# Normalising finished rows on VectorE inside the second attention, and splitting the output weights there in pieces

## The chip, the cores and the metric

The kernel runs as one program on one core of a Trainium2 chip. The metric is the device time of one execution in microseconds (us). Three runs of the kernel before gave a median of 2710.52 us (2707.95 to 2712.14). A change of 0.2% is 5.4 us.

The engines are TensorE (PE, with its weight loads PEld), VectorE (DVE), ScalarE (ACT), GpSimd (POOL) and SyncE (SP). Matrix products are written to PSUM, and DVE or ACT bring them to SBUF. In this kernel DMAs are issued by SP and by POOL.

## The reference

A sequence of 2048 positions with 640 channels passes through four layers, each with a residual: attention, convolution, attention, convolution. Both attentions use the same weights, and both convolutions the same kernel.

```python
x = x + A(layernorm(x), wqkv, wo)   # 32 heads of 20 channels
x = x + B(layernorm(x), ...)        # S4D
x = x + A(layernorm(x), wqkv, wo)
x = x + B(layernorm(x), ...)

A: softmax(q @ k.T * 20 ** -0.5) @ v, heads side by side, @ wo
B: K[d, l] = 2 * Re(sum over n of C[d, n] * exp(A[d, n] * dt[d] * l)), l = 0 .. 2047
   y = irfft(rfft(u, 4096) * rfft(K, 4096))[:2048] + u * D_skip
```

`layernorm` takes mean and variance over the 640 channels of a position, and has no weights.

## The kernel before, in words

A tile of `x` is 128 partitions by 16 rows by 640 channels; "row s" below is one of these 16 (128 positions, 640 channels). Head groups `g` of four heads (8 groups) and query blocks `qb` of 512 positions (4) make the 32 turns of an attention. In a turn, 16 steps over the keys each do two score products on PE (`scores`, line 833), two exponentials of 128x1024 on ACT, and the products with the values on PE (`values`, line 850), which accumulate in `pa`.

**The order of work in an attention is written out by hand.** A `Plan` keeps a clock for PE, ACT and DVE, in units of about one us. After each score product, `fill` puts other pieces of work into PE's gaps as `slot` finds room. A list `later` holds small pieces with a due time, which `drain_later` emits once the plan's PE clock has passed it. While `plan.keep` is set, DVE, ACT, and the DMAs of POOL and SP keep the order in which they were emitted. POOL's arithmetic is not held to that order, and neither is anything behind the attention: there the framework's scheduler sets the order of each engine's queue at build time. Each queue runs in order.

**End of a turn.** `values` copies `pa` to `oc` on DVE. The last row of each head in `oc` holds the sums of the exponentials. They go out to DRAM (`dn<-oc`), come back spread over 128 partitions (`dr<-dn`), are inverted on DVE, go out (`dn<-dr`) and come back broadcast (`db<-dn`). All these DMAs are issued by POOL. Then `scale` multiplies `oc` by `db` on DVE, and `store` sends the block out (`ot<-oc`, POOL). For most turns `scale` is kept until the end of the next turn (`scaled`); for the last two head groups of the second attention it has the due time `plan.dve + 22`.

**Output weights.** Once the projections are done, `end_jobs` (line 905) calls `prefetch` (line 1076), which loads the output weights in five pieces of 128x640 (`wot`, SP) and splits each into a high and a low part, `woh` and `wol`, with a copy (line 1092) and a subtraction (line 1093) on POOL. In the first attention the load of `x` follows, in four DMAs, the last three of them through `later`. In the second attention `end_jobs` also takes a maximum over partitions on POOL, and four small operations on DVE behind it.

**Rows in the second attention.** Its last eight turns alternate between groups 6 and 7. During them `rows_out` (line 970) begins with the output projection: it loads a part of a row (`otl<-ot`, SP; channel tiles 0 to 2, or 3 and 4), splits it on DVE into `oh` and `ol`, multiplies on PE (line 997, three products for each pair), adds to `x` on DVE, and for a row with both parts done takes the statistics of the norm (`mvx`). Such a row is "whole".

**Behind an attention**, `out_proj` (line 1183) does the remaining rows in order (lines 1210 and 1215), with the split's copy on ACT. It calls `ln` for a pair of rows when they are ready, and in the second attention for one whole row after each step. `ln_u` (line 1098) makes `u`, its f16 high part `uh` (ACT) and its low part `ul` (line 1111: POOL, except for the last row). In the first layer `u` is made on DVE, in the second on ACT. In the first layer `ktransform` (line 1120), the transform of the convolution kernel, is woven in; its constants and its input `kl` are loaded by SP. Then `ssm` runs the convolution, whose first stage (line 1279) reads `uh` and `ul`.

Of the kernel before, what the change touches and what calls it, by code (L numbers as in the profile page):

```python
# [21 lines left out]
P = 128  # L22
L = 2048
D = 640
NI = L // P
NCT = D // P
# [11 lines left out]
LG = 2  # L38
BOUND = 30.0
SCALE = DH ** -0.5  # L40
EPS = 1e-5
# [45 lines left out]
def mha_s4d_kernel(ctx, tc, x_in, wqkv, wo, lar, aim, cr, ci, ldt, dsk,  # L87
                   c_e1, c_eb, c_f2, c_fa, c_sel, c_lv, c_id, c_sg, c_e16, c_f16, c_id16, out, parts="asas", general=None):
    nc = tc.nc
    plan = Plan()  # L90
# [42 lines left out]
    flag = cp.tile([P, 2], F32, name="flag")  # L133
# [268 lines left out]
    def attention(x, stats):  # L402
# [439 lines left out]
        def values(qb, g, kt, pts, pa):  # L842

            V = Vt[g // 2 % 3]
            plan.on_pe(0.865)
            for r in range(2):
                rows = slice(64 * r, 64 * r + 64)
                for j in range(4):
                    h = 4 * (g % 2) + j
                    chain(te.matmul(pa[r][32 * j:32 * j + 32, :], V[rows, kt, VP * h:VP * h + 32],  # L850
                                    pts[j // 2][rows, 512 * (j % 2):512 * (j % 2) + 512],
                                    start=(kt == 0), stop=(kt == NI - 1), tile_position=(64 * r, 32 * j)))
            if kt == NI - 1:
# [12 lines left out]
                def sums():  # L866
                    for j in range(4):
                        ge.dma_start(rows[j:j + 1, :], oc[32 * j + DH:32 * j + DH + 1, :])

                def load():  # L870
                    ge.dma_start(dr, dn[0, blk])

                def invert():
                    ve.tensor_scalar_max(dr, dr, 1e-30)
                    ve.reciprocal(dr, dr)

                def back():
# [12 lines left out]

                def store():
                    for j in range(4):
                        h = 4 * g + j
                        ge.dma_start(ot[h * DH:(h + 1) * DH, 512 * qb:512 * qb + 512], oc[32 * j:32 * j + DH, :])
                    stored[blk] = plan.pe
                later.extend((plan.dve + n, f) for n, f in (
                    (0.2, sums), (5.0, load), (10.0, invert), (11.0, back), (15.5, spread)))
                later.extend((plan.dve + n, lambda: slow and slow.pop(0)[1]()) for n in (18.0, 21.0, 24.0))
                if first_layer or g < H // 4 - 2:
                    scaled.append(scale)  # L900
                else:
                    later.append((plan.dve + 22.0, scale))
                later.sort(key=lambda e: e[0])

        def end_jobs():

            while filler[0] is not None:
                while slot():
                    pass
                weave(1)  # L910
            if not first_layer:
                wx = sm.tile([P, 2], F32, name="wx")
                ve.reduce_max(wx[:, 0:1], wm, axis=AX.X)
                ge.partition_all_reduce(wx[:, 1:2], wx[:, 0:1], P, bass.bass_isa.ReduceOp.max)
                ve.tensor_max(flag[:, 0:1], flag[:, 0:1], wx[:, 1:2])
                ve.reciprocal(wx[:, 0:1], wx[:, 1:2])
                ve.tensor_scalar_mul(wx[:, 0:1], wx[:, 0:1], 2.0 ** -4)
                ve.tensor_max(flag[:, 0:1], flag[:, 0:1], wx[:, 0:1])
            qc_.close()
            if not first_layer:  # L920
                xpools.pop().__exit__(None, None, None)
            rest = []
            made = prefetch(x, rest)
            later.extend((plan.pe + 8.0 + 3.0 * n, f) for n, f in enumerate(rest))
            later.sort(key=lambda e: e[0])
            return made

# [12 lines left out]
        class Rows:  # L940
# [21 lines left out]
            def pick(self):  # L962
                for c in (3, 0):
                    for item in self.left:
                        s, c0, c1 = item
                        if c0 == c and (c == 0 or all(4 * g + s // 4 in stored for g in (H // 4 - 2, H // 4 - 1))):
                            self.left.remove(item)
                            return item

        def rows_out(rows, x, woh, wol):  # L970

            def ask():
# [1 line left out]
                if item:  # L974
                    rows.load(item)
                return plan.pe + 6.0
            t, done, parts_done = plan.pe + 26.0, [], set()
            while rows.left or rows.loaded:
                yield t, 0.0, False, ()
                if stop:  # L980
# [26 lines left out]
                if s in parts_done:  # L1007
                    stats_of(x, s, rows.mv[:, s, :])
                    rows.whole.add(s)
                parts_done.add(s)  # L1010

        last[0] = None
# [63 lines left out]
    def prefetch(x, rest):  # L1076

        if x is None:
            xp = tc.tile_pool(name="xp", bufs=1, side="right")
            xpools.append(xp)  # L1080
            x = xp.__enter__().tile([P, NI, D], F32, name="x")
            for i in range(0, NI, 4):
                rest.append(lambda i=i: sy.dma_start(x[:, i:i + 4, :], xv[:, i:i + 4, :]))
        c = ExitStack()
        w1 = c.enter_context(tc.tile_pool(name="wo1", bufs=1, side="right"))
        woh = w1.tile([P, NCT, D], F32R, name="woh")
        wol = w1.tile([P, NCT, D], F32R, name="wol")
        with tc.tile_pool(name="wos", bufs=NCT, side="right") as ws:
            for ct in range(NCT):
                wt = ws.tile([P, D], F32, name="wot")  # L1090
                sy.dma_start(wt, wo[ct * P:ct * P + P, :])
                ge.tensor_copy(woh[:, ct, :], wt)
                ge.tensor_sub(wol[:, ct, :], wt, woh[:, ct, :])
        if rest:
            rest.pop(0)()
        return x, c, woh, wol, c.enter_context(tc.tile_pool(name="wo2", bufs=2, side="right"))

    def ln_u(x, i0, n, mvrs, uh, ul, pool, on_act=False):
        mv, rs = mvrs
# [83 lines left out]
    def out_proj(x, woh, wol, rows, first, ln):  # L1183
# [8 lines left out]
        assert whole == list(range(len(whole)))  # L1192
        rows.left.sort()
        feed()
        if whole:
            rsw = rstd(rows.mv[:, :len(whole), :], len(whole), rows.w2, "rsw")
        to_come = {s: 0 for s in range(NI)}
        for s, c0, c1 in rows.left + [e[0] for e in rows.loaded + first]:
            to_come[s] += 1

        def next_whole():
            if whole:
                s = whole.pop(0)
                ln(s, 1, (rows.mv[:, s:s + 1, :], rsw[:, s:s + 1]))
        while first:
            (s, c0, c1), oh, ol = first.pop(0)
            pos = [pst("M", [P, 512], F32, tag="mm", name="po")[:, :320] for _ in range(2)]
# [4 lines left out]
            for hf in range(2):  # L1212
# [18 lines left out]

    def ssm_consts(c):
# [230 lines left out]
    def seq(x, general):  # L1463

        stats = None
        for n in range(0, len(parts), 2):
            with ExitStack() as c:
# [10 lines left out]
                    psum(c3, M=2, T=2, F=2)  # L1478
                else:
                    psum(c3, M=4)  # L1480
                up = c.enter_context(tc.tile_pool(name="up", bufs=1))
                uh = up.tile([P, NI, D], F16, name="uh")
                ul = up.tile([P, NI, D], F16, name="ul")
                consts = ssm_consts(c)
                with ExitStack() as c2:
                    up2 = c2.enter_context(tc.tile_pool(name="up2", bufs=2 + n))

                    def ln(i0, m, mvrs=None):
                        ln_u(x, i0, m, mvrs or ln_stats(lambda i: x[:, i0 + i, :], m), uh, ul, up2, n > 0 and not general)
# [11 lines left out]
                psum(c, M=2, T=2, F=2)  # L1501
                end = n + 2 >= len(parts)
                stats = ssm(x, uh, ul, consts, end)
        return x

    xpools = []
# [81 lines left out]
```

## Time and profile before

| what | value |
|---|---|
| median of 3 runs | 2710.52 us (2707.95 to 2712.14) |
| the profiled execution | 2711.66 us |
| its span, first to last instruction | 2709.8 us |
| mean granted TensorE clock | 0.991 |
| ACT busy / PE busy | 2351.0 us / 2546.7 us |
| DVE busy / POOL busy | 1489.5 us / 849.7 us |

By stages, in us from the span's start: the first attention ends at about 1101, its output projection with the kernel transform reaches to about 1290, the first convolution to about 1499 together with the start of the second attention, which ends at about 2493; the second output projection lasts to about 2565, and the second convolution to the end.

How to read it: a row of a timeline has the start in us, the length in us, the engine, the line, the operation and its tiles, and in brackets the idle time of the engine before it with what ended that. Most helpers appear as line 77. A "q" behind an engine's name stands for its queue: issues of DMAs and waits. "issue" means that the engine waited for nothing that the profile shows.

### The profile page before, as it was taken

Reading aid. Unit: us, or ns where it says so; the run is one execution under the profiler, and the core shown is the slowest. Engines: PE = TensorE matmul, PEld = TensorE weight load, DVE = VectorE, ACT = ScalarE, POOL = GpSimd, SP = SyncE. Lnnn points to the kernel's source line nnn. Section 1 sums busy time; section 2 is a strip of 40 time slices with the busy share of each in tenths; the row PEclk is TensorE's granted clock in tenths of the full one; section 3 lists DMA queues with packets and bytes.
Section 4 is the critical chain, followed back from the end, with each engine's and each line's share of the span. In section 5 each row is a group of like instructions: output and inputs, shape, how many; then the busy total and the mean of one; then the engine's idle time right before and its main releaser. Section 6 shows DMA issues by size and latency. Waiting matters only on the chain.

```text
span 2709.8 us, 115874 instructions
## 1 busy us (share of the span) xinstructions
PE 2546.7 (94%) x50944; PEld 1439.3 (53%) x50944; DVE 1489.5 (55%) x3324; ACT 2351.0 (87%) x2772; POOL 849.7 (31%) x1282
## 2 busy tenths in 40 slices
PE   7899999999999988999999999999999998999798
PEld 3445444444444433777896544454454443444788
DVE  8677877777856992567776333232233221123765
ACT  7799999999999999455655899999999999998564
POOL 1132333232323334300671122222222224222476
PEclk9999999999999999999999999999999999999999
DMA  6522232322221224455542111111121113222365
GB/s 213 173 61 75 63 79 56 80 67 62 65 54 47 55 70 141 149 194 190 185 157 63 49 51 53 51 55 44 46 62 40 51 39 89 66 68 88 105 191 162
DMA packets 186787, 244.48 MB, mean 90 GB/s; under 512 B 43488, under 2 KB 128992, under 8 KB 184480
## 3 DMA queue, kind: packets, MB, share of 16 engines
q1 hardware_dynamic: 149936, 190.38, 22.1%
q0 software_dynamic: 36336, 46.59, 7.6%
q8 instruction: 402, 6.59, 1.0%
q14 instruction: 113, 0.93, 0.1%
HBM read 160.80 MB, written 76.03 MB: 87 GB/s over the span
## 4 chain that ended last, share of the span: by engine, by line
ACT 51%; PE 26%; issue 10%; DVE 7%; DMA 5%; POOL 1%; SPq 0%; ACTq 0%; DVEq 0%; POOLq 0%
ACT pt L77 49%; PE pa L850 4%; PE psy L1324 3%; PE psv L1314 3%; PE S L833 2%; PE psx L1302 2%; PE psx L1279 2%; PE po L1215 1%; PE m L586 1%; PE pst L1289 1%; PE pkf L1169 1%; DMA kop<-ks 1%; PE pq L739 1%; PE pkx L1152 1%; PE po L1210 1%
## 5 line engine op out<-in xcount | busy, mean ns | idle before, releaser
L77 ACT ACTIVATE pt<-S 128x1024 f32<-128x1024 f32 x2048 | 1929.1, 1033 | 48.7 <-PE S L833 35.5
L850 PE MATMUL pa<-pt,V 64*32 64x512 f32 x16384 | 1102.7, 591 | 0.7 <-DVE oc L77 0.6
L833 PE MATMUL S<-qop,kop 61*32 61x512 f16 x16384 | 882.2, 381 | 88.9 <-ACT pt L77 67.9
L833 PEld LDWEIGHTS <-kop 61*32 61x32 f16 x16384 | 367.2, 90 | 746.0 <-issue 620.3
L850 PEld LDWEIGHTS pa<-pt,V 64*32 64x32 f32 x16384 | 315.0, 106 | 73.7 <-issue 9.4
L77 POOL DMA_DIRECT2D dn<-oc x256 | 125.9, 498 | 662.9 <-DVE oc L77 610.2
L77 DVE TENSOR_SCALAR qc<-m 128x512 f32<-128x512 f32 (+1 forms) x68 | 46.8, 689 | 309.5 <-PE m L586 309.5
L77 POOL DMA_DIRECT2D db<-dn x256 | 129.2, 511 | 141.5 <-DMA dn<-dr 138.2
L586 PE MATMUL m<-xh,wh 64*32 64x512 f16 x2560 | 147.7, 379 | 2.2 <-DVE qc L77 2.0
L77 POOL DMA_DIRECT2D ot<-oc x256 | 129.8, 515 | 62.1 <-DVE oc L77 53.6
L586 PE MATMUL m<-xh,wl 64*32 64x512 f16 x2560 | 147.7, 378 | 0.0
L586 PE MATMUL m<-xl,wh 64*32 64x512 f16 x2560 | 146.0, 377 | 0.0
L77 DVE COPY oc<-pa 128x512 f32<-128x512 f32 x64 | 44.2, 690 | 183.4 <-PE pa L850 175.7
L586 PEld LDWEIGHTS <-wh 64*32 64x32 f16 x5120 | 92.6, 94 | 76.0 <-issue 33.5
L1307 POOL TENSOR_TENSOR t<-t,kb 128x512 f32<-128x512 f32 x80 | 101.9, 1275 | 70.2 <-DVE t L77 69.1
L77 ACT COPY xt<-pst 128x1024 f16<-128x1024 f16 x80 | 81.6, 1023 | 46.9 <-PE pst L1289 46.7
L77 POOL DMA_DIRECT2D dn<-dr x64 | 35.7, 558 | 245.9 <-DVE dr L77 236.8
L77 DVE TENSOR_SCALAR V<-m 128x160 f32<-128x160 f32 x64 | 20.7, 324 | 161.1 <-PE m L552 161.1
L77 DVE TENSOR_TENSOR kb<-ktab 128x512 f32<-128x512 f32 x160 | 106.4, 684 | 0.0
L552 PEld LDWEIGHTS <-xh 128*128 128x128 f16 x960 | 79.6, 98 | 48.0 <-issue 32.6
L1308 POOL TENSOR_TENSOR t<-t,t 128x512 f32<-128x512 f32 x78 | 99.2, 1271 | 7.3 <-DVE t L77 1.3
L323 PEld LDWEIGHTS m<-kb,ka 128*32 128x32 f32 x3840 | 61.0, 109 | 72.2 <-issue 56.6
(280 smaller groups left out, 3990.7 us busy)
## 6 DMA issues: line engine op xcount, KB each, us to landing
ka<-kha SPq DMA_DIRECT2D x80, 256.0 KB
kb<-khb SPq DMA_DIRECT2D x80, 256.0 KB
db<-dn POOLq DMA_DIRECT2D x256, 64.0 KB, 2.8
kop<-ks SPq DMA_DIRECT2D x176, 80.0 KB
kpw<-wd POOLq DMA_DIRECT2D x60, 192.0 KB, 4.9
qop<-qs SPq DMA_DIRECT2D x256, 40.0 KB
ot<-oc POOLq DMA_DIRECT2D x256, 40.0 KB, 2.9
kha<-kn SPq DMA_DIRECT2D x20, 512.0 KB
```

Of the source, the lines that this page charges most:

```text
L77: made = f(out, *a, **k)
L323: chain(te.matmul(ps[32 * j:32 * j + 32, c8, :], a[n][:, ch, :], b[n][:, dd, :], start=(n == 0), stop=(n == 2), tile_position=(0, 32 * j)))
L552: chain(te.matmul(ps[:, :n], a_[:, ct, sl], m[:, ct, :], start=(k == 0), stop=(k == 14)))
L586: chain(te.matmul(ps[r][32 * t:32 * t + 32, :], a_[rows, ct, 32 * u:32 * u + 32], m[rows, ct, 512 * v:512 * v + 512], start=(k == 0), stop ...
L833: chain(te.matmul(S[32 * t:32 * t + 32, 512 * r:512 * r + 512], kt_[rows, kc + 32 * t:kc + 32 * t + 32], qt[rows, :], start=True, stop=Tru ...
L850: chain(te.matmul(pa[r][32 * j:32 * j + 32, :], V[rows, kt, VP * h:VP * h + 32], pts[j // 2][rows, 512 * (j % 2):512 * (j % 2) + 512], sta ...
L1279: te.matmul(ps[:, r, i, :], e1[:, e, s, r, :], m[:, s, bs], start=(n == 0), stop=(n == 2))
L1302: te.matmul(px, f2[:, f, :], xt[:, k, :], start=(n == 0), stop=(n == 2))
L1307: ge.tensor_mul(t2, t2, kb)
L1308: (ge if g0 else ve).tensor_add(t1, t1, t2)
L1314: te.matmul(pv[:, g].rearrange("p r i c -> p (r i c)"), t1[:, g * P:g * P + P], fa, start=True, stop=True)
L1324: te.matmul(py[:, i, :], eb[:, 4 * i4 + i, r, :], v[:, r, 4 * i4 + i].rearrange("p g c -> p (g c)"), start=(r == 0), stop=(r == 1))
```

## The change

1. `scale` of the last two groups of the second attention is due at `plan.dve + 27` instead of 22.
2. The four small DVE operations behind the maximum in `end_jobs` go into `later`, six units on.
3. `prefetch` no longer uses POOL. The weights are loaded into the two buffers `otl` that the row loads use. Five pieces `halves`, one every four units, each copy and subtract on DVE, and issue the load of the next but one weight. The DMAs of `x` in the first attention come behind these pieces.
4. `rows_out` begins at 30 units instead of 26.
5. `normalise`: when a row is whole, DVE computes the inverse root from the bits of the variance and three Newton steps, then `u`, `uh` and `ul`. The five pieces are due 1.2 units apart. For this `uh` and `ul` of the second layer are allocated when the weights are.
6. `out_proj` calls `ln` only for rows that are not whole. In the second layer each call comes one step later in program order than before.

```diff
-                    later.append((plan.dve + 22.0, scale))
+                    later.append((plan.dve + 27.0, scale))
...
-                ve.tensor_max(flag[:, 0:1], flag[:, 0:1], wx[:, 1:2])
-                ve.reciprocal(wx[:, 0:1], wx[:, 1:2])
...
+                def bounds():
+                    ve.tensor_max(flag[:, 0:1], flag[:, 0:1], wx[:, 1:2])
...
+                later.append((plan.pe + 6.0, bounds))
...
-            later.extend((plan.pe + 8.0 + 3.0 * n, f) for n, f in enumerate(rest))
+            later.extend((plan.pe + 8.0 + 4.0 * n, f) for n, f in enumerate(rest))
...
+        def normalise(rows, x, s):
+            mv = rows.mv[:, s, :]
+            va, y, t = (sm.tile([P, 1], F32, tag=f"nr{n}", name=f"nr{n}") for n in range(3))
+            uh, ul = ups
+            def first_guess():
+                ve.tensor_scalar_add(va, mv[:, 1:2], EPS)
+                yi = y.bitcast(mybir.dt.int32)
+                ve.tensor_single_scalar(yi, va.bitcast(mybir.dt.int32), 1, ALU.logical_shift_right)
+                ve.tensor_single_scalar(yi, yi, 0x7FFFFFFF, ALU.bitwise_xor)
+                ve.tensor_scalar_mul(y, y, 0.679 * 2.0 ** -65)
+            def newton():
+                ve.tensor_mul(t, y, y)
+                ve.tensor_mul(t, t, va)
+                ve.tensor_scalar(t, t, -0.5, 1.5, ALU.mult, ALU.add)
+                ve.tensor_mul(y, y, t)
+            def parts():
+                u = rows.w2.tile([P, D], F32, bufs=1, name="u")
+                ve.tensor_scalar(u, x[:, s, :], mv[:, 0:1], y, ALU.subtract, ALU.mult)
+                ve.tensor_copy(uh[:, s, :], u)
+                later.append((plan.dve + 0.5, lambda: ve.tensor_sub(ul[:, s, :], u, uh[:, s, :])))
+                later.sort(key=lambda e: e[0])
+            later.extend((plan.dve + 1.2 * (n + 1), f) for n, f in enumerate((first_guess, newton, newton, newton, parts)))
+            later.sort(key=lambda e: e[0])
...
-            t, done, parts_done = plan.pe + 26.0, [], set()
+            t, done, parts_done = plan.pe + 30.0, [], set()
...
+                    normalise(rows, x, s)
...
+        else:
+            upx = tc.tile_pool(name="upx", bufs=1, side="right")
+            xpools.append(upx)
+            upx_ = upx.__enter__()
+            ups[:] = [upx_.tile([P, NI, D], F16, name=f"u{n}x") for n in "hl"]
...
-        with tc.tile_pool(name="wos", bufs=NCT, side="right") as ws:
-            for ct in range(NCT):
-                wt = ws.tile([P, D], F32, name="wot")
-                sy.dma_start(wt, wo[ct * P:ct * P + P, :])
-                ge.tensor_copy(woh[:, ct, :], wt)
-                ge.tensor_sub(wol[:, ct, :], wt, woh[:, ct, :])
+        w2 = c.enter_context(tc.tile_pool(name="wo2", bufs=2, side="right"))
+        staged = []
+        def weights(ct):
+            wt = w2.tile([P, NCT, P], F32, name="otl").rearrange("p t c -> p (t c)")
+            sy.dma_start(wt, wo[ct * P:ct * P + P, :])
+            staged.append(wt)
+        def halves(ct):
+            wt = staged.pop(0)
+            ve.tensor_copy(woh[:, ct, :], wt)
+            ve.tensor_sub(wol[:, ct, :], wt, woh[:, ct, :])
+            if ct + 2 < NCT:
+                weights(ct + 2)
+        for ct in range(2):
+            weights(ct)
         if rest:
             rest.pop(0)()
-        return x, c, woh, wol, c.enter_context(tc.tile_pool(name="wo2", bufs=2, side="right"))
+        rest[:0] = [lambda ct=ct: halves(ct) for ct in range(NCT)]
+        return x, c, woh, wol, w2
...
-        if whole:
-            rsw = rstd(rows.mv[:, :len(whole), :], len(whole), rows.w2, "rsw")
+        due = []
...
             to_come[s] -= 1
+            if due:
+                ln(*due.pop(0))
             if not to_come[s]:
-                if s >= NI - LG:
-                    ln(s, 1)
+                if s >= NI - LG or s % LG and s - 1 in whole:
+                    due.append((s, 1))
                 elif s % LG == LG - 1:
-                    ln(s + 1 - LG, LG)
-            next_whole()
-        while whole:
-            next_whole()
+                    due.append((s + 1 - LG, LG))
+            if due and len(whole) == 0:
+                ln(*due.pop(0))
+        while due:
+            ln(*due.pop(0))
```

More of the change, by code (lines that the diff above doesn't have):

```diff
@@ L914, in end_jobs @@
                 ge.partition_all_reduce(wx[:, 1:2], wx[:, 0:1], P, bass.bass_isa.ReduceOp.max)
-                ve.tensor_max(flag[:, 0:1], flag[:, 0:1], wx[:, 1:2])
-                ve.reciprocal(wx[:, 0:1], wx[:, 1:2])
-                ve.tensor_scalar_mul(wx[:, 0:1], wx[:, 0:1], 2.0 ** -4)
-                ve.tensor_max(flag[:, 0:1], flag[:, 0:1], wx[:, 0:1])
+                def bounds():
+                    ve.tensor_max(flag[:, 0:1], flag[:, 0:1], wx[:, 1:2])
+                    ve.reciprocal(wx[:, 0:1], wx[:, 1:2])
+                    ve.tensor_scalar_mul(wx[:, 0:1], wx[:, 0:1], 2.0 ** -4)
+                    ve.tensor_max(flag[:, 0:1], flag[:, 0:1], wx[:, 0:1])
+                later.append((plan.pe + 6.0, bounds))
             qc_.close()
@@ L1087, in prefetch @@
         wol = w1.tile([P, NCT, D], F32R, name="wol")
-        with tc.tile_pool(name="wos", bufs=NCT, side="right") as ws:
-            for ct in range(NCT):
-                wt = ws.tile([P, D], F32, name="wot")
-                sy.dma_start(wt, wo[ct * P:ct * P + P, :])
-                ge.tensor_copy(woh[:, ct, :], wt)
-                ge.tensor_sub(wol[:, ct, :], wt, woh[:, ct, :])
+        w2 = c.enter_context(tc.tile_pool(name="wo2", bufs=2, side="right"))
[12 more added lines that the diff above has]
+            weights(ct)
         if rest:
             rest.pop(0)()
-        return x, c, woh, wol, c.enter_context(tc.tile_pool(name="wo2", bufs=2, side="right"))
+        rest[:0] = [lambda ct=ct: halves(ct) for ct in range(NCT)]
+        return x, c, woh, wol, w2
+    ups = []
     def ln_u(x, i0, n, mvrs, uh, ul, pool, on_act=False):
@@ L1199, in out_proj @@
             to_come[s] += 1
[L1201 to L1204, printed above, removed]
         while first:
@@ L1480, in seq @@
                     psum(c3, M=4)
-                up = c.enter_context(tc.tile_pool(name="up", bufs=1))
-                uh = up.tile([P, NI, D], F16, name="uh")
-                ul = up.tile([P, NI, D], F16, name="ul")
+                early = n > 0 and not general
+                if early:
+                    uh, ul = ups
+                else:
+                    up = c.enter_context(tc.tile_pool(name="up", bufs=1))
+                    uh = up.tile([P, NI, D], F16, name="uh")
+                    ul = up.tile([P, NI, D], F16, name="ul")
                 consts = ssm_consts(c)
@@ L1486, in seq, with ln @@
                     up2 = c2.enter_context(tc.tile_pool(name="up2", bufs=2 + n))
-                    def ln(i0, m, mvrs=None):
-                        ln_u(x, i0, m, mvrs or ln_stats(lambda i: x[:, i0 + i, :], m), uh, ul, up2, n > 0 and not general)
+                    def ln(i0, m):
+                        ln_u(x, i0, m, ln_stats(lambda i: x[:, i0 + i, :], m), uh, ul, up2, early)
                     if general:
@@ L1503, in seq @@
                 stats = ssm(x, uh, ul, consts, end)
+            if early:
+                xpools.pop().__exit__(None, None, None)
         return x
```

## The prediction

> **What bounds the kernel now.** I read the page first, then the waits and timelines of each engine at the four places that the change touches.
>
> ```profile
> span 2709.8 us, 115874 instructions
> PE 2546.7 (94%) x50944; PEld 1439.3 (53%) x50944; DVE 1489.5 (55%) x3324; ACT 2351.0 (87%) x2772; POOL 849.7 (31%) x1282
> L77 ACT ACTIVATE pt<-S 128x1024 f32<-128x1024 f32 x2048 | 1929.1, 1033 | 48.7 <-PE S L833 35.5
> ```
>
> ```profile
> 1143.00:1290.00 147.00, 141.30 (x920) 114.23 (x921) 105.79 (x285) 76.79 (x132) 12.55 (x9) 1.00 0.53 193
> ...
> 2285.00:2493.60 208.60, 200.77 (x3645) 89.72 (x3629) 46.19 (x113) 204.85 (x216) 47.13 (x93) 1.00 0.23 64
> ```
>
> The attentions run at the pace of ACT's exponentials, which waited only 35.5 us for scores in the whole run. In the second block (columns: length, busy time of PE, PEld, DVE, ACT, POOL) the last turns of the second attention have ACT at 204.85 of 208.6 us and DVE at 46.19: DVE has room there, and work off it or on it moves the time only through PE and ACT. In the first output projection with the kernel transform, PE is busy 141.3 of 147 us. So I ask of each part whether it removes an ACT wait in an attention, or shifts the start of something that then runs without slack.
>
> **The one large ACT wait in the second attention, and its cause.**
>
> ```profile
> 2282.91 1.02 ACT L77 ACTIVATE pt<-S 128x1024 f32<-128x1024 f32 x1 [4.52 <-PE S L833]
> 2285.04 5.30 ACT L77 ACTIVATE pt<-S 128x1024 f32<-128x1024 f32 x5 [1.11 <-PE S L833]
> ```
>
> ```profile
> PE m L997 <- DVE ol L77: 3.7, 1, 3.7
> ```
>
> ```profile
> 2269.57 0.18 DVE L77 TENSOR_SCALAR dr<-dr 128x16 f32<-128x16 f32 x1 [25.66 <-DMA dr<-dn]
> ...
> 2279.11 0.69 DVE L77 TENSOR_TENSOR oc<-oc,db 128x512 f32<-128x512 f32 x1 [6.14 <-DMA db<-dn]
> ```
>
> ```profile
> 2240.38 0.72 POOL L1092 CAST woh<-wot 128x640 fp32r<-128x640 f32 x1 [9.32 <-DMA wot<-in_wo]
> 2250.29 1.54 POOL L1093 TENSOR_TENSOR wol<-wot,woh 128x640 fp32r<-128x640 f32 x1 [9.20 <-issue]
> ...
> 2260.46 2.16 POOL L77 DMA_DIRECT2D dn<-oc  x4
> ```
>
> Read backwards: ACT waits 4.52 + 1.11 = 5.63 us for scores; PE stands behind its first product of the row output, 3.7 us; that needs a split on DVE, which is queued behind a scale that waits 6.14 us for `db`; and `db` is late because POOL, whose queue is in order, was at the weights until 2260.46 and only then sent the sums. A large piece of that is not arithmetic: 9.20 us before the first subtraction, in which POOL waits for nothing shown.
>
> ```profile
> L1093 POOLq MODIFY_POOL_CONFIG  x4: 5/8/11, 1022.6 to 2241.2; - x4
> ```
>
> ```profile
> 1029.70 3.56 POOL L1093 TENSOR_TENSOR wol<-wot,woh 128x640 fp32r<-128x640 f32 x2 [7.14 <-issue]
> ```
>
> Both attentions show it: a change of POOL's configuration, then 7.14 or 9.20 us until the first two-operand instruction. It belongs to the first such instruction after the maxima over partitions, whatever that is. I call it the reload.
>
> **Part by part.**
>
> *Weights off POOL, second attention.* The chain of the sums is free, the scale finds `db` landed, the 5.63 us go. DVE takes over five copies and five subtractions:
>
> ```profile
> 1079.68 0.49 DVE L77 CAST oh<-otl 128x640 fp32r<-128x640 f32 x1
> 1080.21 0.82 DVE L77 TENSOR_TENSOR ol<-otl,oh 128x640 fp32r<-128x640 f32 x1
> ```
>
> 5 x (0.49 + 0.82) = 6.6 us, inside the 25.66 us in which DVE sat idle before 2269.57: nothing. SP issues two loads and then three, each behind a DVE piece; what queues behind them on SP are key and query loads of the next turn, and the pieces are four units apart, so nothing as long as DVE isn't blocked. If it is, the next turn's keys are late next. The later starts of `rows_out` (+4), the scales (+5) and `bounds` (out of DVE's way) cost nothing at the end: the same products remain, a few of them behind the attention instead of in it. Term: -5.6, and at least -4.5, the wait directly behind the late split.
>
> *Normalising on DVE.* Sixteen operations of one column, three of 640 columns.
>
> ```profile
> 2494.52 0.17 DVE L77 TENSOR_TENSOR lt<-rs 128x6 f32<-128x6 f32 x1
> ```
>
> ```profile
> L77 DVE TENSOR_SCALAR u<-x,mv,rs x16: 593/610/1627, 1117.1 to 1288.2; 128x640 f32<-128x640 f32 x16
> ```
>
> ```profile
> L77 DVE SCALAR_TENSOR_TENSOR nb<-mvx,rs x6: 151/157/1191, 2496.1 to 2525.8; 128x1 f32<-128x1 f32 x6
> ```
>
> With 0.2 us from one small operation to the next: 3.2 + 0.61 + 0.49 + 0.82 = 5.1 us a row, 31 us for the six whole rows, in a stage where DVE idles 162 us. The cost is only where a piece stands ahead of a split that PE waits for. The largest piece is 0.61 + 0.49 = 1.1 us: between 0 and 6 x 1.1 = 6.6 us. I take 0.8, since the pieces are spread and few will meet a split.
>
> *The reload in the first output projection.* With the weights gone from POOL, its first two-operand instruction is the first `ul`.
>
> ```profile
> 1116.32 2.02 POOL L77 DMA_DIRECT2D db<-dn  x4 [1.41 <-DMA dn<-dr]
> 1118.56 3.06 POOL L1111 TENSOR_TENSOR ul<-u,uh 128x640 f16<-128x640 f32 x2 [0.22 <-ACT uh L77]
> 1122.46 2.03 POOL L77 DMA_DIRECT2D ot<-oc  x4 [0.84 <-DVE oc L77]
> ```
>
> ```profile
> SPq L77 <- DMA ot<-oc: 0.8, 1, 0.8
> ```
>
> ```profile
> 1126.02 0.34 SPq L77 DMA_DIRECT2D e<-in_c_e  x1
> ...
> 1127.87 0.94 SPq L77 DMA_DIRECT2D kl<-kd  x1
> ```
>
> ```profile
> 1141.55 1.14 PE L1144 MATMUL pkt<-ident,kl 128*128 128x128 f32 x8 [1.47 <-issue]
> ```
>
> Two `ul` stand in POOL's queue between the last `db` and the last store of the attention. The reload would begin at 1118.34 and end 7.14 later at 1125.48; two `ul` take 3.06; the store goes at 1128.54 instead of 1122.46: +6.1 us (with 9.20: +8.1). SP waits for that store's landing before it loads `e` and `kl`, the transform's first input, so these shift by as much, then the transform's first transposes at 1141.55, and PE behind them has 5.7 us of gaps in 147. Bounds: 0, if the order puts the store ahead of `ul`; 8.1. This code is untouched in the first layer, so I take +6.1, passed on whole.
>
> *The second output projection.*
>
> ```profile
> 2509.88 1.99 POOL L77 DMA_DIRECT2D db<-dn  x4 [1.41 <-DMA dn<-dr]
> 2513.22 4.15 POOL L1111 TENSOR_TENSOR ul<-u,uh 128x640 f16<-128x640 f32 x3 [1.36 <-ACT uh L77]
> 2518.82 2.03 POOL L77 DMA_DIRECT2D ot<-oc  x4 [1.45 <-DVE oc L77]
> ```
>
> ```profile
> 2523.68 0.93 SPq L77 DMA_DIRECT2D otl<-ot  x2
> ```
>
> ```profile
> 2526.95 1.73 ACT L77 ACTIVATE u<-x,nb,rs 128x640 f32<-128x640 f32 x2
> ...
> 2529.20 0.72 ACT L77 CAST oh<-otl 128x640 fp32r<-128x640 f32 x1
> ```
>
> ```profile
> 2529.95 3.45 DVE L77 TENSOR_TENSOR ol<-otl,oh 128x640 fp32r<-128x640 f32 x2 [0.68 <-ACT oh L77]
> ```
>
> ```profile
> 2531.50 2.58 PE L1210 MATMUL po<-woh,ol 128*128 128x320 f32 x10 [4.62 <-DVE ol L77]
> ```
>
> The last four rows start when the last store has landed and been loaded and split; before, PE waited 4.62 us for them. Without the whole rows, two `u` and one `uh` leave ACT's queue between 2526.95 and the split's copy at 2529.20 (2.25 us), and the subtraction, 1.7 us each in the pair while POOL worked beside it, comes back to 0.82 (0.9): -3.1. Against it the reload: 2511.87 + 9.20 (this layer's own value), two `ul` of 1.4 (the pair; the third was a whole row's), so the store goes at 2523.9 instead of 2518.8: +5.1. Together +2.0, bounds -3.1 (store ahead of `ul`) and 9.20 + 2.8 - 3.1 = +8.9 (the reload stands ahead of a link of the sums' chain). I lean to the middle, because the pair's `ul` stood between `db` and the store.
>
> [...]
>
> **Sum.** -5.6 + 0.8 + 6.1 + 2.0 = +3.3 us. The profiled execution took 2711.66, 1.1 above the median of 2710.52; on the median the change gives 2713.8 us, within 0.2% (5.4 us, about what a measurement can tell from no change).
>
> **Rivals.**
> - *Both reloads hide.* The stores stand ahead of the first `ul`, and the reload falls into POOL's idle time: -5.6 + 0.8 + 0 - 3.1 = -7.9, 2702.6. For it: `ln` comes a step later in the second layer. Against it: in the first layer nothing moves, and there the order was `db`, `ul`, `ul`, store.
> - *Only the first hides:* -5.6 + 0.8 + 2.0 = -2.8, 2707.7.
> - *Slower: the reload gets ahead of a link of the sums' chain* in the second output projection (before `db` or `dn<-dr`): -5.6 + 0.8 + 6.1 + 8.9 = +10.2, 2720.7. It makes the kernel slower by more than 5.4 us as soon as the second projection loses over 4.1 us. For it: with less on ACT and DVE the pair may come earlier in the order. Against it: the pair came after `db` before.
> - *Slower: the normalising pieces meet the splits,* every time: -5.6 + 6.6 + 6.1 + 2.0 = +9.1, 2719.6. DVE's 162 idle us speak against it.
>
> **How the numbers follow.** Forecast 0.45, of which 0.31 stay within 5.4 us and 0.14 (reload nearer 9.2 in the first layer, or a little more from the pieces) are slower. Both hide: 0.18, all but 0.01 faster. Only the first hides: 0.10, of which 0.08 the same and 0.02 faster. Chain link: 0.13 slower. Pieces: 0.10, 0.08 slower and 0.02 the same. Unseen: 0.04, 0.03 slower and 0.01 faster. Faster 0.20, same 0.42, slower 0.38. The range goes from the case in which both hide to a little beyond the chain-link case, 2702 to 2722; the forecast's own is 2709 to 2719.
>
> **What would show it.** Attention: no ACT wait over 2 us at the first row products, and no wait of DVE for `db` there. Reload: the configuration change stands at line `ul` and an idle stretch of 7 to 9 us on POOL before the first `ul` in each projection; the first store at about 1128.5, `kl` and the first `pkt` 6 us later, and the stretch from there to the first convolution as long as before. Second projection: PE on the last four rows about 2 us later after the attention's end. I am wrong if POOL's order differs from before, if the transform catches up, or if DVE makes PE wait in the last turns.

## The result and the profile after

The changed kernel takes 2717.67 us (median of 7 runs, 2712.74 to 2723.47), the kernel before 2707.95 us beside it (7 runs, 2704.55 to 2712.14). The ratio is 1.0033, with a 95% interval of 1.0019 to 1.0046: 8.9 us slower, by more than the 0.2% that can be told from no change. The profiled execution took 2717.67 us, its span is 2715.8 us. ACT's waits for scores in the attentions fell, and the time rose all the same:

```profile
span 2715.8 us, 115958 instructions
PE 2544.0 (94%) x50944; PEld 1439.2 (53%) x50944; DVE 1521.7 (56%) x3458; ACT 2341.9 (86%) x2756; POOL 816.9 (30%) x1255
...
L77 ACT ACTIVATE pt<-S 128x1024 f32<-128x1024 f32 x2048 | 1929.6, 1032 | 41.6 <-PE S L833 26.9
```

**The stall in the second attention is gone.** In the timeline of ACT there is no wait at the first row products, where 4.52 and 1.11 us were lost before, and DVE's scale comes to a `db` that has landed:

```profile
2283.31 7.61 ACT L77 ACTIVATE pt<-S 128x1024 f32<-128x1024 f32 x8
```

```profile
2280.65 0.69 DVE L77 TENSOR_TENSOR oc<-oc,db 128x512 f32<-128x512 f32 x1
```

From the start of the 1801st exponential to the end of the last, the stretch is 239.46 us, and was 244.74: -5.3.

**The reload is now in both output projections.** The configuration change stands at the line of `ul` (1160 after the change), and POOL's timeline has the idle stretch behind it, 7.75 us in the first layer, 6.97 in the second. What the brackets name there, a load and a product, is no input of `ul`; ACT was done with its inputs by 1118.85 and 2513.16.

```profile
L1160 POOLq MODIFY_POOL_CONFIG  x4: 37/37/37, 1118.2 to 2512.4; - x4
```

```profile
1116.07 2.02 POOL L77 DMA_DIRECT2D db<-dn  x4 [1.41 <-DMA dn<-dr]
1125.84 1.40 POOL L1160 TENSOR_TENSOR ul<-u,uh 128x640 f16<-128x640 f32 x1 [7.75 <-DMA otl<-ot]
1127.21 2.31 POOL L77 DMA_DIRECT2D ot<-oc  x4
...
2511.73 0.55 POOL L77 DMA_DIRECT2D dn<-dr  x1 [4.20 <-DVE nb L77]
2519.25 1.40 POOL L1160 TENSOR_TENSOR ulx<-u,uhx 128x640 f16<-128x640 f32 x1 [6.97 <-PE po L1258]
2520.61 2.20 POOL L77 DMA_DIRECT2D db<-dn  x4
2523.15 2.77 POOL L1160 TENSOR_TENSOR ulx<-u,uhx 128x640 f16<-128x640 f32 x2 [0.34 <-ACT uhx L77]
2527.74 2.04 POOL L77 DMA_DIRECT2D ot<-oc  x4 [1.82 <-DVE lt L77]
```

In the first layer the last store goes at 1127.21 (1122.46 before). In the second the first `ul` now stands ahead of `db`, so that the reload holds up a link of the sums' chain: `db` goes 25.8 us after the last exponential, and 17.4 us before. PE then waits 11.58 us for the last four rows (4.62 before). In the first layer the kernel transform's input is loaded 4.9 us later than before, and its first transposes come 7.4 us later:

```profile
1130.99 0.35 SPq L77 DMA_DIRECT2D e<-in_c_e  x1
...
1132.81 0.83 SPq L77 DMA_DIRECT2D kl<-kd  x1
```

```profile
1148.98 2.99 PE L1193 MATMUL pkt<-ident,kl 128*128 128x128 f32 x12 [2.65 <-issue]
...
2536.36 3.03 PE L1253 MATMUL po<-woh,ol 128*128 128x320 f32 x10 [11.58 <-DVE ol L77]
```

The two stages as blocks (length, then busy time of PE, PEld, DVE, ACT, POOL), from the end of an attention's last exponential to the first copy of transposed rows in the convolution; first the kernel before, then the changed one:

```profile
1100.07:1298.83 198.76, 187.01 (x1261) 157.04 (x1260) 144.42 (x376) 93.41 (x161) 30.88 (x33) 0.98 0.55 198
...
2492.44:2564.93 72.49, 56.77 (x457) 53.36 (x454) 54.05 (x136) 38.93 (x66) 28.58 (x29) 0.93 0.33 103
```

```profile
1099.90:1308.54 208.64, 188.52 (x1261) 158.19 (x1260) 147.18 (x376) 93.79 (x159) 31.84 (x33) 0.97 0.53 189
...
2494.77:2570.94 76.17, 57.93 (x461) 55.19 (x458) 48.94 (x142) 29.05 (x48) 20.36 (x26) 0.87 0.32 99
```

So the stages give -5.3 in the attention, +9.9 in the first projection with the transform, +3.7 in the second projection: +8.3 us, against +8.9 by the ratio. (The two spans differ by only 6.0 us: the profiled execution of before had waits of some 3 us of its own, see the last experiment.)

### The profile page after: what moved, and what is told of

It reads as the page before. It is cut to its first block, busy times and chain, and to the rows that moved or that the text cites. A ratio compares the mean times of both kernels' runs of the same rounds, so it can differ in the third digit from the quotient of the medians.

```text
span 2715.8 us, 115958 instructions
## 1 busy us (share of the span) xinstructions
PE 2544.0 (94%) x50944; PEld 1439.2 (53%) x50944; DVE 1521.7 (56%) x3458; ACT 2341.9 (86%) x2756; POOL 816.9 (30%) x1255
## 4 chain that ended last, share of the span: by engine, by line
ACT 49%; PE 26%; issue 13%; DVE 6%; DMA 5%; POOL 1%; SPq 0%; ACTq 0%; DVEq 0%; POOLq 0%
ACT pt L77 48%; PE pa L850 4%; PE S L833 3%; PE psv L1360 3%; PE psy L1370 2%; PE po L1258 2%; PE psx L1348 2%; PE psx L1325 2%; DMA kop<-ks 1%; PE m L586 1%; PE po L1253 1%; PE pst L1335 1%; PE pkf L1218 1%; PE pkx L1201 1%; DVE ktab L77 1%
## 5 line engine op out<-in xcount | busy, mean ns | idle before, releaser
L77 ACT ACTIVATE pt<-S 128x1024 f32<-128x1024 f32 x2048 | 1929.6, 1032 | 41.6 <-PE S L833 26.9
L77 POOL DMA_DIRECT2D ot<-oc x256 | 130.4, 517 | 50.9 <-DVE oc L77 44.4
```

Source lines behind the costliest of these rows:

```text
L77: made = f(out, *a, **k)
```

## Experiments

Every time below has its ratio to the kernel before, measured on the same chip beside it, except the last run's. Theory R: the loss is the reload, by what stands behind it in POOL's queue. The rivals blame the work that was moved.

### The reload moved into the attention

`early` is a two-operand instruction on POOL of one column. It pulls the reload to a place behind a broadcast of the sums, where POOL idled 15 to 17 us in the changed kernel.

```
 def end_jobs():
+    wake.append(1)            # e1: both layers; e2: first; e3: second
 ...
 def spread():                 # behind the four issues of db
+    if wake:
+        wake.pop()
+        e = sm.tile([P, 1], F32, name="early")
+        ge.last = tie(ge.tensor_sub(e, ident[:, 0:1], ident[:, 1:2]), ge.last)
```

> The changed kernel plus one two-operand instruction of 128 elements on POOL in each attention, behind a broadcast of the sums, so that the reload falls where POOL idles 15 to 17 us. Theory R (the reload at the first ul in each output projection is the loss): the first transform starts 7.4 us earlier and ends 9.7 us earlier than in the changed kernel, PE's wait for the last four rows in the second projection (11.58 us) falls below 5, and the time is 2700 to 2703 us, ratio to before 0.997 to 0.998. Rival D (the loss comes from the work that was moved to DVE and from its later places, the reload falls into idle time): within 2 us of the changed kernel, 2716 to 2719, ratio 1.0025 to 1.004.

Measured 2701.06 us, ratio 0.9965 (0.9953 to 0.9978): as R has it, and faster than both kernels. POOL's timeline shows the reload in the attentions, and in the projections no idle stretch ahead of `ul`:

```profile
1074.39 0.18 POOL L888 TENSOR_TENSOR early<-ident 128x1 f32<-128x1 f32 x1 [11.87 <-issue]
...
1121.06 2.02 POOL L77 DMA_DIRECT2D db<-dn  x4 [1.41 <-DMA dn<-dr]
1123.34 3.01 POOL L1168 TENSOR_TENSOR ul<-u,uh 128x640 f16<-128x640 f32 x2 [0.27 <-ACT uh L77]
1127.20 2.03 POOL L77 DMA_DIRECT2D ot<-oc  x4 [0.84 <-DVE oc L77]
...
2266.30 0.19 POOL L888 TENSOR_TENSOR early<-ident 128x1 f32<-128x1 f32 x1 [10.48 <-issue]
...
2504.75 2.02 POOL L77 DMA_DIRECT2D db<-dn  x4
```

The first stage takes 196.9 us (208.64 in the changed kernel), the second 71.47 (76.17). PE still waits 7.88 us for the last four rows, not under 5 as expected: the store waits there 5.09 us for the scale on DVE.

```profile
1104.80:1301.70 196.90, 186.87 (x1261) 156.93 (x1260) 144.13 (x376) 93.51 (x159) 30.88 (x33) 0.98 0.55 200
...
2485.81:2557.28 71.47, 57.89 (x461) 55.14 (x458) 50.23 (x142) 28.86 (x49) 20.81 (x26) 0.88 0.34 105
```

> The same instruction in the first attention alone. R: the transform of the first layer ends 9.7 us earlier, the second projection still has its wait of 11.6 us on PE: 2707 to 2709 us, ratio 1.000. D: 2716 to 2719.

Measured 2706.22 us, ratio 0.9985 (0.9976 to 0.9994), 1 us below what R gives. The first stage is 198.2 us, and PE's wait in the second projection is still 12.77 us: the first layer's part alone.

> The same instruction in the second attention alone. R: the first transform keeps its delay of 9.7 us; in the second projection the broadcast of the last reciprocals goes at about 2514 instead of 2520.6 us of the changed kernel's clock, PE waits 4 to 5 us instead of 11.58 for the last four rows, 2710 to 2712 us, ratio 1.001. D: 2716 to 2719.

Measured 2716.06 us, ratio 1.0023 (1.0014 to 1.0031). The first stage stays at 208.6 us, the second falls to 70.3, and PE's wait to 7.88 us. D's time fits here, but its stages don't: the 5.9 us won in the second projection are spent elsewhere. In the profiled execution the stages up to the end of the second attention took 3.8 us more than in the changed kernel (1.3 up to the end of the first attention, 0.7 from there to the last turns of the second, 1.8 in these turns, where ACT waits 1.53 us for scores 5 us behind the early instruction). That wait needs no reload beside it: the run with the first instruction alone, whose second attention has none, waits 1.03 us at the same place, and with both instructions there is no wait. One execution of each doesn't tell more.

### The same one instruction in the kernel before

```
 ge.partition_all_reduce(wx[:, 1:2], wx[:, 0:1], P, bass.bass_isa.ReduceOp.max)
+e = sm.tile([P, 1], F32, name="early")
+ge.last = tie(ge.tensor_sub(e, ident[:, 0:1], ident[:, 1:2]), ge.last)
```

> The kernel before, weights still on POOL, with the small instruction directly behind the last maximum over partitions of the second attention, where POOL then waits 9.3 us for the weights to land. Theory R: the reload of 9.2 us is what made the sums late; POOL is through with the weights at 2251 instead of 2260.5, the scale no longer waits for its broadcast, the wait of 4.5 and 1.1 us of ACT goes: 2702 to 2703 us, ratio 0.998. Rival W (the 11 us of copies and subtractions are enough to make the sums late): 2707 to 2709, ratio 1.000.

Measured 2700.97 us, ratio 0.9962 (0.9949 to 0.9974). The reload runs while POOL waits for the weights anyway; the copies and subtractions are still on POOL, and the sums go out at 2248.56. From the 1801st exponential that is 5.0 us, and 12.8 before. ACT's waits for scores over the last turns, 5.6 us before, are not there:

```profile
2226.20 0.32 POOL L77 PARTITION_ALL_REDUCE wx<-wx  x1
2236.72 0.18 POOL L916 TENSOR_TENSOR early<-ident 128x1 f32<-128x1 f32 x1 [10.20 <-DMA wot<-in_wo]
2236.87 0.71 POOL L1094 CAST woh<-wot 128x640 fp32r<-128x640 f32 x1
...
2248.56 2.16 POOL L77 DMA_DIRECT2D dn<-oc  x4
```

The stretch of the last turns is 238.6 us, as short as in the changed kernel. So the stall that the change removes was the reload's; the 11 us of arithmetic alone did not cause it, and one instruction of 0.18 us removes it whole. The ratio is better than the 0.998 expected: it stands for some 10 us, of which 6.2 are in these turns. Where the rest lies one execution doesn't tell. The changed kernel with both early instructions takes the same time (2701.06 us, 0.9965). So with the reload out of the way, nothing else in the change shows a worth in the total.

### The reload left in the projections, but behind the store

```
-(ve if s == NI - 1 else ge).tensor_sub(ul[:, s, :], u, uh[:, s, :])
+made = (ve if s == NI - 1 else ge).tensor_sub(ul[:, s, :], u, uh[:, s, :])
+if s < NI - 1 and floor is not None:   # floor: POOL's last store of the attention
+    tie(made, floor)
```

> The changed kernel without any early instruction, but with every ul of the output projections ordered on POOL behind the last store of the attention, so that both reloads stay in the projections and fall behind the store. Theory R (a reload costs only by what stands behind it in POOL's queue): the stores go at 1120 to 1123 us in the first layer (1127.2 in the changed kernel), the transform ends 8 to 10 us earlier, the broadcast in the second projection goes at about 2514 and PE's wait for the last four rows falls from 11.6 to 4 to 8 us: 2700 to 2706 us, ratio 0.997 to 0.999. Rival (a reload in the projections costs wherever it stands, since the ul behind it are late and the rows' transform waits for them): 2713 to 2718.

Measured 2702.61 us, ratio 0.9979 (0.9969 to 0.9988), as R has it. The idle stretches are still in the projections, with nothing urgent behind them:

```profile
1121.85 2.02 POOL L77 DMA_DIRECT2D ot<-oc  x4 [2.92 <-DVE oc L77]
1131.31 2.78 POOL L1160 TENSOR_TENSOR ul<-u,uh 128x640 f16<-128x640 f32 x2 [7.45 <-ACT oh L77]
...
2507.44 2.01 POOL L77 DMA_DIRECT2D db<-dn  x4 [1.41 <-DMA dn<-dr]
2514.00 2.01 POOL L77 DMA_DIRECT2D ot<-oc  x4 [4.55 <-DVE oc L77]
2522.94 7.50 POOL L1160 TENSOR_TENSOR ulx<-u,uhx 128x640 f16<-128x640 f32 x5 [6.92 <-ACT oh L77]
```

The stages are 200.1 and 67.6 us. The last turns of the attention take 243.3 us in this execution: ACT waits 4.2 us for scores there, four times and up to 1.6 us, with one late load of queries on PE.

The same ordering on top of the early instructions, and, in the first layer alone, on the kernel before with its early instruction:

> Both early instructions, and the ul of the projections behind the last store. Theory R adds nothing for the reload here; what goes is the 3.0 us of two ul between the last broadcast and the store in the first layer, and 1.4 us of one ul ahead of the broadcast in the second: 2696 to 2699 us, ratio 0.995 to 0.996. Rival (the transform's start is set by the loads of rows and constants on SP, not by the store): 2700 to 2702, as with the early instructions alone.

> The kernel before with the early instruction in the second attention (weights on POOL, no normalising on DVE, the old times), and in the first layer alone the ul behind the last store. If the change's own parts (normalising, weights on DVE, later times) are worth something once the reload is out of the way, this is slower than the same two edits on the changed kernel by their worth, 1 to 3 us: 2698 to 2700. If they are worth nothing, the two are equal within 1 us.

Measured 2705.08 us, ratio 0.9988 (0.998 to 0.9997), and 2704.6 us, ratio 0.9981 (0.9972 to 0.999). Both are slower than without the ordering (0.9965 and 0.9962), which nothing expected had. Between the two the intervals overlap, so here too the rest of the change shows no worth. With both edits on the changed kernel the first stage is 199.47 us instead of 196.9; on the kernel before it is 201.5 instead of 197.4. In the changed kernel the store goes 21.1 us behind the attention's last exponential, and 22.4 with the early instructions alone; the load of `e` goes 24.7 us behind it, and 26.0:

```profile
1124.10 0.35 SPq L77 DMA_DIRECT2D e<-in_c_e  x1
```

So the store is earlier by only 1.3 us, and that brings the transform nothing. The traces show why: the first transposes start when DVE has added `skip` to `kl`, and in both kernels `kl` had landed before DVE came to that (landed 37.7 us behind the last exponential and added at 41.0 with the early instructions alone, 37.5 and 42.1 with the ordering). Where a part of the added time comes from is visible too. While POOL runs the first two `ul`, a DVE operation of two columns lasts to their end, 2.65 us instead of 0.16, and PE waits 1.70 us for the addition behind it:

```profile
1122.58 2.78 POOL L1168 TENSOR_TENSOR ul<-u,uh 128x640 f16<-128x640 f32 x2
```

```profile
1122.74 2.65 DVE L77 TENSOR_TENSOR lt<-rs 128x2 f32<-128x2 f32 x1
```

The kernel before with the ordering has the same 2.65 us. Without the ordering the pair ran beside the scale, which took 1.57 us instead of 0.69. The first transposes come 1.2 us later with the ordering; where the rest of the 2.6 us comes from was not settled.

### The normalising undone

The six rows are normalised in the projection again, with both early instructions in place:

```
 if s in parts_done:
     stats_of(x, s, rows.mv[:, s, :])
     rows.whole.add(s)
-    normalise(rows, x, s)
...
-    due.append((s, 1))                       # out_proj as in the kernel before
+    next_whole()
```

> Both early instructions, but the six finished rows are normalised in the projection on ACT, DVE and POOL, as before the change; weights on DVE and the later times stay. The prediction's step has these rows cost 3.1 us of PE's wait in the second projection: the stretch from the last exponential to the first copy of transposed rows is 72.5 us with both early instructions and becomes 75 to 76, the attention is unchanged within 1 us, 2703 to 2706 us. Rival (the normalising pieces on DVE delay the last turns by as much as they save behind them): 2700 to 2702, and the last turns of the attention 1 us or more shorter.

Measured 2699.19 us, ratio 0.9962 (0.9951 to 0.9973), against 0.9965 with the normalising. The second projection takes 70.97 us (71.47 with it), the last turns 239.35 us (239.20). The expected 3 us are not there in either stage: as far as these times tell (either ratio is known to about 3 us), the normalising on DVE costs nothing and brings nothing.

### Eight rows ahead of the transform, or nine

In the build of the changed kernel nine rows (270 products) of the first output projection stand on PE ahead of the transform's first transposes; in the kernel before, and in every kernel here without the reload ahead of the first store, eight (240). The scheduler sets this when it builds the program. The edit holds PE to eight and leaves POOL's order, with the reload, untouched:

```
+mark.append(te.transpose(...).ins)           # the first transpose of kl
 ...
 made = te.matmul(pos[hf], ol[:, ct, :], woh[:, ct, 320 * hf:320 * hf + 320], ...)
+if s == 8 and mark:
+    tie(made, mark.pop())
```

> The changed kernel with its reload in place and POOL's order untouched; only the first products of the ninth row of the first output projection are ordered on PE behind the first transposes of the kernel transform, so that eight rows (240 products) stand ahead of the transform as in the kernel before, and not nine (270). Theory O (in the first layer the compiled order that goes with the reload's place is the loss, since PE is busy nearly throughout): from the last exponential of the first attention to the first copy of transposed rows 198 to 202 us instead of 208.6, the time 2707 to 2711 us. Theory W (the delayed store and the loads behind it on SP, as the prediction has it): 207 to 209 us there, the time 2715 to 2719.

Measured 2709.7 us, ratio 1.0002 (0.9991 to 1.0013), a time as theory O has it. The stage takes 204.27 us, between the two theories, and PE now visibly waits for DVE's addition of `skip` to `kl`, which stands behind the `u` of two rows in DVE's queue:

```profile
1144.10 3.85 PE L1195 MATMUL pkt<-ident,kl 128*128 128x128 f32 x16 [4.14 <-DVE kl L77]
```

```profile
1098.03:1302.30 204.27, 188.92 (x1261) 158.38 (x1260) 146.53 (x376) 93.65 (x160) 31.21 (x33) 0.97 0.53 193
```

```profile
1142.80 1.14 DVE L77 TENSOR_SCALAR u<-x,mv,rs 128x640 f32<-128x640 f32 x2
1143.85 0.15 DVE L77 TENSOR_TENSOR kl<-kl,skip 128x1 f32<-128x1 f32 x1
```

Both have a part: of the 9.9 us, 4.4 (208.64 - 204.27) go with the ninth row, and 5.5 (204.27 - 198.76) with the reload's place. The split is rough, since the stage takes 196.9 to 199.25 us in the kernels here that have neither the delay nor the ordering of the `ul`.

Nor are the 5.5 us all the loads' delay. Behind the last exponential, `kl` landed at 44.4 us here and at 38.5 in the kernel before, 5.9 later. But there DVE added `skip` only at 41.2, 2.7 us after the landing, and here at 45.8. So of the 4.6 us by which the first transposes are later, at most 3.2 (44.4 - 41.2) are the loads', and 1.4 are DVE's order. Of the total's 8.4 us the stage explains 4.4; 2.0 more lie in the second projection (74.22 us) and 1.9 in the first attention of the profiled execution, where the edit has no part.

### The old times, and the kernel before once more

```
-later.append((plan.dve + 27.0, scale))      +later.append((plan.dve + 22.0, scale))
-later.append((plan.pe + 6.0, bounds))       +bounds()
-plan.pe + 8.0 + 4.0 * n                     +plan.pe + 8.0 + 3.0 * n
-t, done, parts_done = plan.pe + 30.0        +t, done, parts_done = plan.pe + 26.0
```

> Both early instructions in the changed kernel, with the old places in the order: scaling 22 units behind, row output 26, weight pieces 3 apart, the bound's four instructions at once. If the later times matter (the scale reaches DVE before its broadcast has landed), ACT waits 1 to 6 us at the first row products of the second attention and the time is 2702 to 2707 us. If they don't, once the reload is out of the queue, the last turns stay within 1 us of 238.2 and the time at 2699 to 2702.

Measured 2696.64 us, ratio 0.9949 (0.9934 to 0.9964), the fastest here. ACT waits for nothing at the row products, the last turns take 238.26 us, and the second projection 69.0: in this build `db` stands ahead of the first `ul`, and PE's wait for the last four rows is 2.28 us:

```profile
2517.16 2.76 PE L1261 MATMUL po<-woh,ol 128*128 128x320 f32 x10 [2.28 <-DVE ol L77]
```

So the later times were not needed once the reload was out of the way. In these executions they cost 1 us in the attention and, by another order, 2.5 in the projection; whether they cost anything in the total stays open, since the intervals of the two ratios overlap (0.9934 to 0.9964, and 0.9953 to 0.9978 with the later times).

> The kernel before unchanged, for one more profile. In the first profile ACT waits 2.69, 0.68 and 0.76 us for scores at 1766 to 1772 us, which no other kernel here shows, with identical instructions there. If that is chance of one execution, the sixteen exponentials around it take 15.3 us here as in the others, not 18.6, and the stall of 5.6 us at the first row products stays. If it belongs to the kernel before, 18 to 19 us come again, and 3 to 4 us of every difference to it are from there.

One execution: 2713.32 us. The stretch of sixteen exponentials (from the start of the first to that of the last) takes 14.58 us, and 18.59 in the other execution; the waits at 1766 us do not come back, the stall at the first row products does (4.16 and 1.11 us):

```profile
1770.39 10.47 ACT L77 ACTIVATE pt<-S 128x1024 f32<-128x1024 f32 x11 [0.38 <-PE S L833]
```

```profile
2284.47 1.02 ACT L77 ACTIVATE pt<-S 128x1024 f32<-128x1024 f32 x1 [4.16 <-PE S L833]
```

It was chance of one execution. In exchange this one's first attention ended at 1104.56, 4.5 us later than in the other, with the same instructions; 1.35 of these lie ahead of its first exponential.

## Why the prediction was right and where it was wrong

The main mechanism was right: the stall is the reload's, and the change does not remove the reload but moves it to the first `ul` of each projection. What it costs there was not: the forecast was +3.3 us, within 0.2%, and +8.9 was measured. The time lies in the range, above the forecast's 2713.8 us; that it comes near the chain-link rival's 2720.7 is partly luck, since the first projection cost 3.8 us more than that rival has and the second 5.2 less. One sign of being wrong that the prediction names came true in both projections: POOL's order differs from before (one `ul` and not two ahead of the first layer's store, a `ul` ahead of the second's `db`). Point by point:

- **The stall, -5.6:** -5.3 measured. That `db` was late because of POOL is shown by the kernel before with the early instruction. The prediction had the cure as "weights off POOL"; the weights could have stayed.
- **Normalising, +0.8:** 0.15 in the last turns (239.35 without it, 239.20 with it, so if anything in its favour). In the changed kernel PE's only wait for a split in the last turns is 0.3 us. DVE's spare time covered it, as argued.
- **First projection, +6.1, "passed on whole":** +9.9, the step that was mis-sized. The idle stretch was 7.75 us (7.14 taken), the store went 4.75 us later and not 6.1, since one `ul` and not two stood ahead of it. With eight rows held ahead of the transform 5.5 us of the loss stay; the other 4.4 go with the ninth row on PE. The prediction took this code as untouched and so its order as fixed; but behind the attention the scheduler sets the order anew, and wherever it was left free here, nine rows came with a reload ahead of the first store and eight without. How the scheduler comes to that isn't shown. "Passed on whole" was wrong too. The chain from store to loads to transposes left out that before the change `kl` had landed 2.7 us before DVE added `skip` to it: the transposes waited for DVE's turn, not for the load. The later landing accounts for at most 3.2 us; the order on DVE and PE made up for the slack and more.
- **Second projection, +2.0:** +3.7. The rival of the slower side, a reload ahead of a chain link, is what happened there: `db` 8.4 us later after the attention. Its price of +8.9 was too high by 5.2. The reload took 6.97 us and not 9.20. From `db` to the store it was 7.1 us, and 8.9 before; from the store to PE's products 8.6, and 12.7 before, since ACT had no rows queued ahead of the split. So PE began the last four rows only 2.5 us later, 41.6 us behind the last exponential and 39.1 before. The shorter way from the store is the -3.1 that the prediction gave for it, here 4.1.
- **The claim that this saving is the normalising's** failed: with the early instructions in place the second projection was as short without the normalising (70.97 us, 71.47 with it), and from the store to PE's products it took 9.6 us without it and 10.9 with it.
- **The sum:** -5.6 + 0.8 + 6.1 + 2.0 = +3.3 stood against -5.3 + 0 + 9.9 + 3.7 = +8.3. Most of the difference is the first projection's 3.8 us. The bound for it, 8.1, was set by the reload's longest duration and so held only the delay, not another order.

## What to carry to other kernels

When work is taken off an in-order queue, ask which one-off cost was paid by its first instruction, and who will pay it next (here 9.20 us ahead of the first subtraction of the weights, then 6.97 ahead of the first `ul`); a tiny instruction of the same kind, put where the queue idles, was worth more here (0.9962 on the kernel before) than the whole rearrangement (1.0033). Where a scheduler sets the order at build time, another order can come with a moved cost (here nine rows on PE ahead of the transform and not eight, 4.4 us): compare the two programs' orders on the busiest engine, not just the delays. Before passing on a delay whole, look how long the delayed thing lay ready before it was used (`kl` 2.7 us before the change). Judge a part by its stage in the trace, and with care, since two executions of the same program differed by 4 us in single stretches.

## What was not expected of the hardware

- The reload's length differs with where it runs; why, and what POOL does in it, stays open. The idle stretch ahead of the instruction that met it was 6.92 to 7.75 us in the output projections (7.75 and 6.97 in the changed kernel, 7.45 and 6.92 with the store first, 7.54 with eight rows), and 9.63 to 11.87 us ahead of `early` in an attention (11.87 and 10.48 with both instructions, 9.63 with the second alone, 10.20 in the kernel before); ahead of the weights on POOL it was 7.14 in the first attention and 9.20 in the second.
- Two executions of the kernel before, with the same instructions, differ by 4 us in a stretch of sixteen exponentials (18.59 and 14.58 us), and by 4.5 us up to the end of the first attention, the other way round.
- An earlier store on POOL, with the `ul` behind it, made the first stage 2.6 us longer (199.47 against 196.90). While its first two `ul` ran, a DVE operation of two columns took 2.65 us and not 0.16; the rest of the loss stays open.
